# Attention and a gated MLP on one core: a new table of planned times, first loads placed one by one, and the last 128 tokens summed in two PSUM banks

## The chip, the cores and the metric

The kernel runs on one core of one Trainium2 chip. The metric is the device time of one execution in microseconds; the median of several executions counts. The engines are TensorE (PE; its weight loads are shown apart as PEld), VectorE (DVE), ScalarE (ACT), GpSimd (POOL) and SyncE (SP, which here only issues transfers).

## What is computed

Windowed causal attention (each position sees itself and the 63 before it), then a two-layer MLP whose hidden layer is gated by the sigmoid of a convolution of three taps along the sequence. Batch 8, 8 heads, 576 positions, 64 per head; 512 model columns, 1024 hidden ones.

```python
def _attn_ref(q, k, v):                       # q, k, v: 8 x 8 x 576 x 64
    scores = np.matmul(q, k.transpose(0, 1, 3, 2)) / np.sqrt(D)
    mask = (rel >= 0) & (rel < 64)            # rel = query position - key position
    scores = np.where(mask, scores, -1e9)
    scores = scores - np.max(scores, axis=-1, keepdims=True)
    attn = np.exp(scores)
    attn = attn / (np.sum(attn, axis=-1, keepdims=True) + 1e-09)
    return np.matmul(attn, v)

def _moe_ref(x, w_in, conv_w, w_out):         # x: 8 x 576 x 512
    h = np.maximum(x @ w_in, 0.0)             # w_in: 512 x 1024
    conv_out = sum(conv_w[k] * shifted(h, k - 1) for k in range(3))
    gate = 1.0 / (1.0 + np.exp(-conv_out))
    return h * gate @ w_out                   # w_out: 1024 x 512
```

The three MLP weights arrive as 64-bit floats; the kernel reads them as pairs of 32-bit words and makes 32-bit floats of them itself.

## The kernel before

**Units.** The 4608 tokens are worked off in 12 units (`NU`) of 384 tokens. For each unit PE does, in this order of dependence:

- *scores* (`qk`, L375): k and q of six blocks of 64 tokens. In the first two units the score blocks are 64 rows high, from the third on 32. A batch of the later units is 64 or 128 pairs of weight load and multiply as the trace counts them; DVE adds the mask and takes the row maximum (`row_max`, L382), ACT does the exponentials (`exps`, L392), then the rows are normalised (L403);
- a transpose of the probabilities (first two units on PE, L408, copied out by ACT, L413; later units on DVE, L429, and through transfers `ub<-T`, L441);
- *values* (`values`, L527): four groups per unit, each 12 matmuls in the program and 24 in the trace (a 32-bit matmul takes two passes), into one of three PSUM banks `acc`. ACT and DVE then split the sum into a rounded high part `xh` (L531) and a remainder `xl` (L534), and only after that is the bank free;
- the *first layer* (`mm1`, L547): per hidden block `f` of 128 (8 per unit) 12 matmuls of 384 columns (high by high, low by high, high by low, over four slices), into an `acc` bank; ACT takes the positive part (`relu`);
- the convolution and the gate on ACT and DVE (L582 to L616), two hidden blocks at a time;
- the *second layer* (`mm2`, L624): per hidden block 9 matmuls of 512 columns, three for each 128 tokens (`o` = 0, 1, 2), each `o` with a bank `po` of its own in which all eight hidden blocks are summed.

**The stream on PE.** In the steady part mm1 of unit u and mm2 of about two units back alternate, 12 matmuls and 9, and the scores and values of later units are put between them.

**The start.** SP issues the loads of k and q of unit 0, of v, and the weight words (`bits`, 512 KB each). While PE waits at the start it runs fillers (`keep_busy`, L222): matmuls on a zero tile whose results nobody reads. Each weight piece is made into a 32-bit float by two ACT operations (L259, L264) and three or four on DVE (L260, L261, L265, L283).

**The end.** After the last mm2, the bank of `o` = 2 is copied out in two halves, one by DVE and one by ACT (L660), and SP issues one transfer for each (L661).

**What sets the order.** All work is entered in a list with `at(t, engine, cost, ...)`. `queued` (the planner, L58 on) then simulates the five engines with the given costs: among the ready works of an engine it takes the one with the smallest planned time `t`, and the order so found is the order in which the instructions are issued. The planned times come from the table `START` and from the unit's number. Where PE has nothing to do before 110 us of planned time, `queued` puts in as many fillers as it thinks fit into the gap. Nothing of the planner runs on the chip: its costs decide the order and the fillers alone.

## Time and profile before

| what | value |
|---|---|
| median of 3 runs | 508.39 us (508.06 to 509.17) |
| the profiled execution, its own time | 507.84 us |
| its span, first to last instruction | 506.1 us |
| PE busy | 497.7 us, 98% of the span, fillers counted |
| DVE busy | 368.6 us, 73% |
| ACT busy | 384.5 us, 76% |
| POOL busy | 92.3 us, 18% |
| granted TensorE clock | 1.000 |

A busy share counts fillers, and a matmul whose end overlaps the next counts once. So the share of PE says that PE hardly ever stands still, not that all it does is needed. The time that a stretch of PE costs is read from start to start: from the start of its first matmul to the start of the next stretch's first. In the chain of waits each row is a stretch of one kind (start, us, engine, tile, line, count).

### The profile page before, as it was taken

What the parts mean: (1) busy time and instruction counts of PE and PEld (TensorE: products, weight loads), DVE (VectorE), ACT (ScalarE), POOL (GpSimd) and SP (SyncE); (2) the same over time, 40 slices, a digit from 0 to 9 for tenths busy, and PEclk for the clock granted to TensorE, in tenths of its full rate; (3) what the DMA queues carried; (4) which work ended last, traced back from release to release, by engine and by line L of the source; (5) the groups of instructions that cost most, each with busy time, mean ns of one, the idle gap of its engine ahead of it and who ended that gap; (6) DMA issues with size and microseconds to landing.
All of it is one profiled execution on the core that took longest, in us unless ns stands there. A gap on an engine that the chain in (4) does not pass through costs nothing.

```text
span 506.1 us, 14072 instructions
## 1 busy us (share of the span) xinstructions
PE 497.7 (98%) x5428; PEld 445.5 (88%) x5428; DVE 368.6 (73%) x1079; ACT 384.5 (76%) x1012; POOL 92.3 (18%) x196
## 2 busy tenths in 40 slices
PE   9999999999999999999999999999999999999996
PEld 8888998989989989988988997998998998999885
DVE  4999999795796777767677676695877585454970
ACT  6999998969979869949958956966975984444750
POOL 7125321301121402102100420220210230000000
PEclk9999999999999999999999999999999999999999
DMA  8986833629127226316415522712720521100111
GB/s 289 384 314 220 319 112 110 221 72 321 35 67 280 91 68 239 114 48 219 152 48 177 188 55 92 268 50 82 278 56 18 194 60 31 63 0 1 63 64 62
DMA packets 28163, 69.89 MB, mean 138 GB/s; under 512 B 5696, under 2 KB 15680, under 8 KB 28096
## 3 DMA queue, kind: packets, MB, share of 16 engines
q1 hardware_dynamic: 28096, 68.99, 40.0%
q8 instruction: 43, 0.70, 0.6%
q14 instruction: 24, 0.20, 0.1%
HBM read 47.73 MB, written 9.44 MB: 113 GB/s over the span
## 4 chain that ended last, share of the span: by engine, by line
PE 84%; ACT 7%; DVE 4%; SPq 1%; DMA 1%; issue 1%; POOL 0%; ACTq 0%; POOLq 0%
PE po L624 36%; PE acc L547 36%; PE acc L527 6%; ACT s L392 4%; PE sc L375 3%; PE acc L375 2%; DVE s L382 1%; SPq L441 1%; DMA q<-in_q_dram 1%; ACT L392 1%; ACT c L582 1%; DVE T L261 1%; ACT L596 1%; DVE T L265 0%; DVE c L589 0%
## 5 line engine op out<-in xcount | busy, mean ns | idle before, releaser
L589 DVE SCALAR_TENSOR_TENSOR c<-hbuf,cw,c 128x384 f32<-128x384 f32 (+1 forms) x192 | 116.9, 657 | 26.3 <-ACT c L582 25.6
L547 PE MATMUL acc<-xh,wih 128*128 128x384 f32 x384 | 131.1, 341 | 1.0 <-DVE nm L382 1.0
L547 PE MATMUL acc<-xl,wih 128*128 128x384 f32 x384 | 129.4, 337 | 0.0
L547 PE MATMUL acc<-xh,wil 128*128 128x384 f32 x384 | 128.9, 336 | 0.0
L624 PE MATMUL po<-woh,gh 128*128 128x512 f32 x288 | 114.2, 397 | 0.0
L624 PE MATMUL po<-wol,gh 128*128 128x512 f32 x288 | 113.4, 394 | 0.0
L624 PE MATMUL po<-woh,gl 128*128 128x512 f32 x288 | 111.9, 389 | 0.0
L392 ACT ACTIVATE s<-s,nm 128x96 f32<-128x96 f32 (+2 forms) x288 | 105.4, 372 | 3.4 <-DVE nm L382 3.2
L547 PEld LDWEIGHTS acc<-xh,wih 128*128 128x128 f32 x384 | 72.1, 188 | 6.8 <-DVE nm L382 1.0
L547 PEld LDWEIGHTS acc<-xh,wil 128*128 128x128 f32 x384 | 72.1, 188 | 2.7
L547 PEld LDWEIGHTS acc<-xl,wih 128*128 128x128 f32 x384 | 72.1, 188 | 0.0
L403 POOL TENSOR_TENSOR s<-s,r 128x768 f32<-128x768 f32 x27 | 41.4, 1532 | 159.0 <-DVE r L398 116.5
L624 PEld LDWEIGHTS po<-woh,gl 128*128 128x128 f32 x288 | 54.1, 188 | 12.2
L601 DVE TENSOR_TENSOR c<-c,hbuf 128x768 f32<-128x768 f32 (+1 forms) x48 | 46.2, 963 | 22.3 <-ACT c L596 21.9
L624 PEld LDWEIGHTS po<-woh,gh 128*128 128x128 f32 x288 | 54.0, 187 | 9.6
L624 PEld LDWEIGHTS po<-wol,gh 128*128 128x128 f32 x288 | 54.2, 188 | 7.6
L576 ACT ACTIVATE hbuf<-acc 128x384 f32<-128x384 f32 x64 | 30.9, 486 | 38.4 <-PE acc L547 38.4
L582 ACT ACTIVATE c<-hbuf,cw 128x384 f32<-128x384 f32 (+1 forms) x96 | 53.8, 610 | 7.0 <-DVE gl L616 6.9
L616 DVE TENSOR_TENSOR gl<-c,gh 128x768 fp32r<-128x768 f32 x48 | 45.7, 952 | 16.2 <-ACT gh L613 16.0
L392 ACT ACTIVATION_READ_ACCUMULATOR s<-s,nm 128x1 f32 x288 | 55.5, 193 | 0.0
L613 ACT CAST gh<-c 128x768 fp32r<-128x768 f32 x48 | 39.8, 831 | 13.6 <-DVE c L601 7.9
L596 ACT ACTIVATE c<-c 128x768 f32<-128x768 f32 (+1 forms) x48 | 40.7, 847 | 3.9 <-DVE c L589 3.1
(72 smaller groups left out, 578.9 us busy)
## 6 DMA issues: line engine op xcount, KB each, us to landing
v<-in_v_dram SPq DMA_DIRECT2D x24, 768.0 KB, 6.5
ub<-T SPq DMA_DIRECT2D x240, 48.0 KB, 1.9
k<-in_k_dram SPq DMA_DIRECT2D x22, 448.0 KB, 6.1
q<-in_q_dram SPq DMA_DIRECT2D x22, 384.0 KB, 6.4
out_dram<-T SPq DMA_DIRECT2D x11, 768.0 KB, 3.6
bits<-in_w_in_dram SPq DMA_DIRECT2D x8, 512.0 KB, 7.8
bits<-in_w_out_dram SPq DMA_DIRECT2D x8, 512.0 KB, 4.1
k<-in_k_dram SPq DMA_DIRECT2D x2, 256.0 KB, 4.6
```

The lines of the kernel that those rows point to most:

```text
L392: nc.scalar.activation(x, x, AF.Exp, bias=nms[b][:, e], scale=-1.0, accum_out=sms[b][:, e])
L403: on.tensor_tensor(sv, sv, rs[b][:, e].unsqueeze(2).broadcast_to([P, e.stop - e.start, n]), ALU.mult)
L527: nc.tensor.matmul(acc[bank(("v", u, c))][h * D:(h + 1) * D, t * W:(t + 1) * W], vs[:, c, t, h], ub[g][:, 2 * p:2 * p + 2, 2 * t + h], sta ...
L547: nc.tensor.matmul(acc[bank(("m", u, f))][:, :NX], w[:, f, c], x[u % 2][:, c], start=(c == 0 and j == 0), stop=(c == NC - 1 and j == 2))
L576: nc.scalar.activation(hbuf[:, f, 1:1 + NX], ps[:, :NX], AF.Relu)
L582: nc.scalar.activation(cs[i % 2][:, a, :n], hbufs[u % 2][:, f, 1:1 + n], AF.Copy, scale=cw[:, 1, f:f + 1])
L589: nc.vector.scalar_tensor_tensor(c, hbufs[u % 2][:, f, e:e + n], cw[:, e, f:f + 1], c, op0=ALU.mult, op1=ALU.add)
L596: nc.scalar.activation(c, c, AF.Sigmoid)
L601: nc.vector.tensor_tensor(c, c, hbufs[u % 2][:, 2 * i:2 * i + 2, 1:1 + n], ALU.mult)
L613: nc.scalar.copy(halves(u, ghs[ring(u, i)]), kept(u, cs[i % 2]))
L616: nc.vector.tensor_tensor(halves(u, gls[ring(u, i)]), kept(u, cs[i % 2]), halves(u, ghs[ring(u, i)]).bitcast(F32), ALU.subtract)
L624: nc.tensor.matmul(po[t], x, w[:, f], start=(f == 0 and j == 0), stop=(f == NF - 1 and j == 2))
```

## The change

**The planner's model.** `queued` now counts how many PE instructions are waiting to be run: the kinds "tiled" (scores of the first two units and values) and "eight" (scores of the later units) use up a store of at most 170 units that fills up again at 12 per us; where the store is empty the planned end is put later. Some costs are lowered (ACT's weight operations, the copies, the gate), a few are raised, and the size put down for a load of k, q and v in the first units is smaller.

**The table.** All numbers of `START` are new. `sig`, `pv`, `ex`, `qk` and `mid` have a row more (units 0 to 3 and the rest), and `first` gives each of the four first pairs of k and q loads a time of its own.

**The last unit.** For `o` = 2 of the last unit, `mm2` is done in two halves of 256 columns, into the bank `po[2]` and the bank `sc[0]`. The last two hidden blocks are put in order of `o`: both blocks for `o` = 0, then both for 1, then both for the two halves of 2. DVE copies the half in `po[2]` and SP issues its transfer; ACT copies the half in `sc[0]` and issues that transfer itself.

```diff
@@ queued
-        end = free[e] = start + turn + x.cost * (1.75 if e == "PE" and start < WARM else 1.0)
+        end = start + turn + x.cost * (1.75 if e == "PE" and start < WARM else 1.0)
+        if e == "PE" and x.kind:
+            n = FEED[x.kind] * x.cost
+            fed = min(FEED_CAP, fed + (start - fed_at) * FEED_RATE)
+            end += max(0.0, (n - fed) / FEED_RATE - (end - start))
+            fed, fed_at = fed + (end - start) * FEED_RATE - n, end
+        free[e] = end
@@ START
-    "qk0": (-97.809, -91.941, -91.937, -96.905, -77.255, -53.129),
+    "first": (-93.058, -80.147, -81.455, -79.474),
+    "qk0": (-63.31, -62.834, -53.48, -26.846, -47.703, -53.065),
...
+FEED, FEED_CAP, FEED_RATE = {"tiled": 33, "eight": 78}, 170.0, 12.0
@@ load_qk
+                t = START["first"][2 * g + a] if u == 0 else t
...
-                       w=[(name, g, n) for n in range(i, j)], mb=(0.00145 if u == 0 else 0.00112) * (e.stop - e.start))
+                       w=[(name, g, n) for n in range(i, j)], mb=(0.0012 if u == 0 else 0.0009 if u == 1 else 0.00112) * (e.stop - e.start))
@@ to_f32 (the other costs are changed in the same way)
-        at(t, "ACT", 0.0009 * n + 0.2, lambda: nc.scalar.activation(x, hw.bitcast(F32), AF.Abs, scale=2.0 ** -112), r=kb, w=kt)
+        at(t, "ACT", 0.0009 * n + 0.11, lambda: nc.scalar.activation(x, hw.bitcast(F32), AF.Abs, scale=2.0 ** -112), r=kb, w=kt)
@@ mm2
-    def mm2(u, f, t):
+    def mm2(u, f, t, half=None):
...
+        ps, e = (po[t], slice(0, DM)) if half is None else last_part(half)
         for j, (x, w) in enumerate(((gh, woh), (gh, wol), (gl, woh))):
-            nc.tensor.matmul(po[t], x, w[:, f], start=(f == 0 and j == 0), stop=(f == NF - 1 and j == 2))
+            nc.tensor.matmul(ps[:, :e.stop - e.start], x, w[:, f, e], start=(f == 0 and j == 0), stop=(f == NF - 1 and j == 2))
+
+    def last_part(half):
+        return (po[TT - 1], sc[0])[half], slice(half * DM // 2, (half + 1) * DM // 2)
@@ moe
+                if u == LAST and f >= NF - 2:
+                    t = n0 + NF - 2 + START["lag"][min(u, 5)] + 0.5 + 0.02 * o + 0.004 * (f - NF + 2)
...
-                for eng, cost, cut, copy in (("ACT", 0.35, slice(0, DM // 2), nc.scalar.copy), ("DVE", 0.35, slice(DM // 2, DM), nc.vector.tensor_copy)):
-                    at(t + 0.05 * o, eng, cost, lambda cut=cut, copy=copy: copy(ot[:, TT - 1, cut], po[TT - 1][:, cut]), r=[("po", o)], w=[("ot", o, cut.start)])
-                    at(t + 0.05 * o + 0.01, "SP", 0.45, lambda cut=cut: nc.sync.dma_start(out[u, :, TT - 1, cut], ot[:, TT - 1, cut]), r=[("ot", o, cut.start)], mb=0.13)
+                for half, key, eng, copy in ((0, ("po", o), "DVE", nc.vector.tensor_copy), (1, ("sc", 0), "ACT", nc.scalar.copy)):
+                    ps, e = last_part(half)
+                    at(t + 0.05 * o + 0.01 * half, eng, 0.4, lambda e=e, ps=ps, copy=copy: copy(ot[:, o, e], ps[:, :DM // 2]),
+                       r=[key], w=[("ot", o, half)])
+                    issue, by = ((nc.sync, "SP"), (nc.scalar, "ACT"))[half]
+                    at(t + 0.05 * o + 0.01 * half + 0.005, by, 0.45, lambda e=e, issue=issue: issue.dma_start(out[u, :, o, e], ot[:, o, e]),
+                       r=[("ot", o, half)], mb=0.13)
```

What this does to the order is shown at three places. The first is SP, its first transfers, before:

```order
L273 DMA bits_102<-in_w_in_dram 128x1024
L304 DMA cbits<-in_conv_w_dram 128x48
L245 DMA k<-in_k_dram 128x2x192
L245 DMA q<-in_q_dram 128x2x128
L245 DMA k<-in_k_dram 128x2x256
L245 DMA q<-in_q_dram 128x2x256
L245 DMA k<-in_k_dram 128x2x192
L245 DMA q<-in_q_dram 128x2x128
```

And SP's first transfers now:

```order
L255 DMA k<-in_k_dram 128x2x192
L255 DMA q<-in_q_dram 128x2x128
L283 DMA bits_102<-in_w_in_dram 128x1024
L255 DMA k<-in_k_dram 128x2x192
L255 DMA q<-in_q_dram 128x2x128
L255 DMA k<-in_k_dram 128x2x256
L255 DMA q<-in_q_dram 128x2x256
L255 DMA k<-in_k_dram 128x2x256
```

The first small pair of k and q now goes ahead of the first weight piece, the second small pair goes ahead of the large ones, and the words of the convolution (`cbits`) come later.

The second place is PE in a unit of the steady part (`ub` holds the transposed probabilities, `sc` and `acc` are banks). Before, a batch of 128 score pairs is followed by one group of values and then the second layer; the other three groups follow 21 matmuls later:

```order
L375 MATMUL sc_105<-k,q 32x96
L375 MATMUL sc_106<-k,q 32x96
L527 MATMUL acc_109<-ub_61,v 64x64 x12
L624 MATMUL po_110<-woh,gh_97 128x512
L624 MATMUL po_110<-wol,gh_97 128x512
L624 MATMUL po_110<-woh,gl_100 128x512
```

Now the four groups of values stand together, and the batch of 128 score pairs (64 rows of the order) follows at once:

```order
L635 MATMUL po_112<-woh,gl_100 128x512
L537 MATMUL acc_108<-ub_61,v 64x64 x12
L537 MATMUL acc_109<-ub_61,v 64x64 x12
L537 MATMUL acc_107<-ub_62,v 64x64 x12
L537 MATMUL acc_108<-ub_62,v 64x64 x12
L385 MATMUL sc_105<-k,q 32x96
L385 MATMUL sc_106<-k,q 32x96
```

The first and the fourth group use the same bank. The batch of 64 score pairs, which followed the three groups before, now stands alone between mm1 and mm2 stretches. Six units have this form.

The third place is the end of PE's program, before (`po_110`, `po_111`, `po_112` are `o` = 0, 1, 2):

```order
L624 MATMUL po_110<-woh,gl_100 128x512
L624 MATMUL po_111<-woh,gh_97 128x512
L624 MATMUL po_111<-wol,gh_97 128x512
L624 MATMUL po_111<-woh,gl_100 128x512
L624 MATMUL po_112<-woh,gh_97 128x512
L624 MATMUL po_112<-wol,gh_97 128x512
L624 MATMUL po_112<-woh,gl_100 128x512
```

And now:

```order
L635 MATMUL po_111<-woh,gl_100 128x512
L635 MATMUL po_112<-woh,gh_97 128x256
L635 MATMUL po_112<-wol,gh_97 128x256
L635 MATMUL po_112<-woh,gl_100 128x256
L635 MATMUL po_112<-woh,gh_97 128x256
L635 MATMUL po_112<-wol,gh_97 128x256
L635 MATMUL po_112<-woh,gl_100 128x256
L635 MATMUL sc_105<-woh,gh_97 128x256
L635 MATMUL sc_105<-wol,gh_97 128x256
L635 MATMUL sc_105<-woh,gl_100 128x256
L635 MATMUL sc_105<-woh,gh_97 128x256
L635 MATMUL sc_105<-wol,gh_97 128x256
```

`o` = 1 is done twelve narrow matmuls before the end instead of three wide ones, and the last half has a bank of its own. Over the whole program PE has 44 fillers instead of 50 (rows of `keep_busy`, two passes each), 18 stretches of values instead of 27, and 840 wide and 48 narrow matmuls of the second layer instead of 864 wide ones.

More of the change, by code (lines that the diff above doesn't have):

```diff
@@ L97, in queued @@
             waiting[x.eng].append(x)
-    dma, port, order, left = 0.0, {"DVE": 0.0, "POOL": 0.0}, [], len(works)
+    dma, fed, fed_at = 0.0, FEED_CAP, 0.0
+    port, order, left = {"DVE": 0.0, "POOL": 0.0}, [], len(works)
     while left:
@@ L274, in weights @@
                 bits[buf][:, a * DM:(a + 1) * DM], src[f].bitcast(U32).rearrange("p (e two) -> p e two", two=2)),
-               w=[("bits", buf, a)], mb=0.52)
+               w=[("bits", buf, a)], mb=0.52 if key == "out" else 0.46)
         n = len(fs) * DM
@@ L279, in weights @@
         if key == "out":
-            at(t, "ACT", 0.0009 * n + 0.12, lambda: nc.scalar.copy(hi, x), r=kt, w=his)
+            at(t, "ACT", 0.00088 * n + 0.05, lambda: nc.scalar.copy(hi, x), r=kt, w=his)
         else:
-            two(t, "POOL", 0.00127 * n, lambda: nc.gpsimd.tensor_copy(hi, x), r=kt, w=his)
+            two(t, "POOL", 0.00105 * n, lambda: nc.gpsimd.tensor_copy(hi, x), r=kt, w=his)
         two(t, "DVE", 0.00104 * n + 0.07, lambda: nc.vector.tensor_tensor(lo, x, hi.bitcast(F32), ALU.subtract), r=kt + his, w=los)
@@ L477, in weigh @@
             at(t + 0.4, "PE", 0.66, lambda n=n: transpose_pe(u, n), r=[("s", b, n % 2 * 2), ("s", b, n % 2 * 2 + 1), "mask0"], w=m)
-            at(t + 0.5, "ACT", 0.55, lambda n=n: untile(u, n), r=m, w=[("u", g, i) for i in range(4)])
+            at(t + 0.5, "ACT", 0.47, lambda n=n: untile(u, n), r=m, w=[("u", g, i) for i in range(4)])
     def softmax(u, b, t, ex_at):
@@ L498, in softmax @@
             at(t, "DVE", 0.15, lambda: guard(b, e, nc.vector), w=sw)
-        at(t, "DVE", 0.15, lambda: reciprocal(b, e), r=sw, w=[("r", b, i) for i in range(NB)])
+        at(t, "DVE", 0.12, lambda: reciprocal(b, e), r=sw, w=[("r", b, i) for i in range(NB)])
         if u < 3:
@@ L537, in attend @@
         g, x = c // 2, u % 2
-        at(t, "PE", 0.72, lambda: values(u, c), r=[("v", g)] + [("u", g, i) for i in range(4)], w=[("acc", ("v", u, c))],
+        at(t, "PE", 0.735, lambda: values(u, c), r=[("v", g)] + [("u", g, i) for i in range(4)], w=[("acc", ("v", u, c))],
            kind="tiled")
-        at(t + 0.1, "ACT", 0.4, lambda: split_hi(u, c), r=[("acc", ("v", u, c))], w=[("xh", x, c)])
+        at(t + 0.1, "ACT", 0.375, lambda: split_hi(u, c), r=[("acc", ("v", u, c))], w=[("xh", x, c)])
         at(t + 0.2, "DVE", 0.48, lambda: split_lo(u, c), r=[("acc", ("v", u, c)), ("xh", x, c)], w=[("xl", x, c)])
@@ L634, in moe @@
                    w=[("acc", ("m", u, f))])
-            at(n + 0.3, "ACT", 0.4, lambda f=f: relu(u, f), r=[("acc", ("m", u, f))], w=[("h", y, f)])
+            at(n + 0.3, "ACT", 0.385, lambda f=f: relu(u, f), r=[("acc", ("m", u, f))], w=[("h", y, f)])
             for o in range(TT):
-                at(n + START["lag"][min(u, 5)] + 0.5 + 0.01 * o, "PE", 0.683, lambda f=f, o=o: mm2(u, f, o),
-                   r=[("gh", ring(u, f // 2)), ("gl", ring(u, f // 2)), f"out{f}h", f"out{f}l"],
-                   w=[("po", o)])
+                t = n + START["lag"][min(u, 5)] + 0.5 + 0.01 * o
+                if u == LAST and f >= NF - 2:
+                    t = n0 + NF - 2 + START["lag"][min(u, 5)] + 0.5 + 0.02 * o + 0.004 * (f - NF + 2)
+                r = [("gh", ring(u, f // 2)), ("gl", ring(u, f // 2)), f"out{f}h", f"out{f}l"]
+                if u == LAST and o == TT - 1:
+                    for half in range(2):
+                        at(t + 0.01 * half, "PE", 0.36, lambda f=f, o=o, half=half: mm2(u, f, o, half), r=r,
+                           w=[(("po", o), ("sc", 0))[half]])
+                    continue
+                at(t, "PE", 0.683, lambda f=f, o=o: mm2(u, f, o), r=r, w=[("po", o)])
         for i in range(NF // 2):
```

62 lines of the change are left out of this document (31 added, 31 removed), and 6 rows, old and new, of the table START.

## The prediction

> **What bounds the kernel now.** I read the page's busy shares first, then the busy time by stretches, then PE's own rows from start to start, and the chain of waits for the steady part.
>
> ```profile
> span 506.1 us, 14072 instructions
> PE 497.7 (98%) x5428; PEld 445.5 (88%) x5428; DVE 368.6 (73%) x1079; ACT 384.5 (76%) x1012; POOL 92.3 (18%) x196
> ...
> q8 instruction: 43, 0.70, 0.6%
> ```
> ```profile
> 0.00:20.00 20.00, 18.19 (x219) 16.59 (x220) 12.56 (x66) 15.05 (x60) 10.72 (x46) 1.00 0.91 331
> 20.00:40.00 20.00, 19.37 (x310) 16.79 (x307) 19.89 (x69) 18.63 (x58) 4.19 (x7) 1.00 0.84 297
> 40.00:60.00 20.00, 19.24 (x363) 17.68 (x364) 19.93 (x73) 19.25 (x73) 10.14 (x15) 1.00 0.84 305
> ```
> ```profile
> L222 PE MATMUL acc<-spare 128*128 128x112 f32 x78 | 12.3, 317 | 1.1 <-DVE spare L225 1.1
> L222 PE MATMUL po<-spare 128*128 128x112 f32 x12 | 2.2, 296 | 0.0
> L222 PE MATMUL sc<-spare 128*128 128x112 f32 x10 | 1.6, 293 | 0.0
> ```
>
> In the second fence the columns are stretch, length, busy time of PE, PEld, DVE, ACT, POOL, clock, share and rate of the transfers. PE is the bound, so three things can save time: gaps on PE, fillers that stand for gaps, and what PE loses between kinds of matmul. The fillers (100 rows, 12.3 + 2.2 + 1.6 = 16.1 us) lie nearly all in the first 40 us, where DVE is full from 20 us on (19.89 and 19.93 of 20) and ACT nearly so.
>
> ```profile
> 274.98 2.30 PE acc L547 x12
> ...
> 306.00 0.79 PE acc L527 x21
> 306.79 1.06 issue
> 307.86 0.33 PE acc L527 x3
> ...
> 315.73 2.31 PE acc L547 x12
> ...
> 351.99 2.25 PE acc L527 x72
> 354.24 0.93 PE sc L375 x58
> 355.17 2.31 PE acc L547 x12
> 357.47 2.06 PE po L624 x9
> 359.53 2.11 PE acc L547 x12
> ```
>
> The chain of waits (start, us, what, rows) shows the steady part. From 315.73 to 355.17 one unit takes 39.44 us. The unit before took 40.75 us (274.98 to 315.73), and the 1.31 us more are one gap inside a group of values, where PE waited for nothing but its own instructions ("issue"). Everywhere else PE runs without a break from about 47 us to the last matmul at 501.70.
>
> **The change part by part.** The terms are against the profiled execution, 507.84 us, which lies 0.55 us under the median of the runs (508.39).
>
> *The start.*
>
> ```profile
> 0.74 0.38 SPq L273 DMA_DIRECT2D bits<-in_w_in_dram  x1
> ...
> 1.64 0.43 SPq L245 DMA_DIRECT2D k<-in_k_dram  x1
> ...
> 4.40 0.67 ACT L259 ACTIVATE T<-bits 128x512 f32<-128x512 f32 x1 [2.38 <-DMA bits<-in_w_in_dram]
> ...
> 5.07 0.68 ACT L264 ACTIVATE bits<-bits 128x512 uint32<-128x512 uint32 x1
> ...
> 6.18 0.57 PE L375 MATMUL sc<-k,q 64*64 64x64 f32 x16 [0.17 <-DMA q<-in_q_dram]
> ...
> 7.17 0.35 ACT L392 ACTIVATE s<-s,nm 128x64 f32<-128x64 f32 x1 [1.30 <-DVE nm L382]
> ```
> ```profile
> bits<-in_w_in_dram SPq DMA_DIRECT2D x8, 512.0 KB, 7.8
> ```
>
> The first scores start when the first q has landed, behind 512 KB of weights. Now that pair goes first: 512 KB less at 331 GB/s (first stretch) is **1.6 us** earlier. PE's program agrees: six fillers fewer, 12 rows of 0.16 us (16.1 us over 100), 1.9 us. ACT gains less. Its first weight operation still stands ahead of the first exponentials, and its words now land behind k and q, by about 1.0 us (128 x 2 x 192 and 128 x 2 x 128 floats are 320 KB, at the same rate; or two issues of 0.43 us), so it ends near 6.1; exponentials start about 1.0 us before 7.17, and the second weight operation (0.68 us), which had lain in idle time, now lies among them: 0.4 us gained. The ends are 0.4 and 1.9 us. I take 1.6, because PE's rows are what ends here, and because DVE, idle for 7.4 of the first 20 us, can start its full stretch as much earlier.
>
> *Stretches of values.* 72 rows take 2.25 us (351.99 to 354.24); 48 take 1.55:
>
> ```profile
> 88.41 1.55 PE acc L527 x48
> ```
>
> So 24 rows cost 0.70 us and each stretch 0.15 us besides. Nine stretches fewer (18 for 27) save 1.35 us, and one return to wide matmuls less saves its surplus, 2.31 against 2.11, 0.2 us: **1.5 us**. The number of excursions from the wide matmuls per steady unit is unchanged, so nothing more comes of it. From below this is 0: the fourth group of values now needs the bank of the first, and waits if ACT's and DVE's split takes over 2.25 us.
>
> *Instructions for PE.* Blocks of instructions are brought by the transfers of q8 (packets, MB, share): 43 for 2 x 5428 rows, so some 256 each. I counted PE's instructions in program order (a 32-bit matmul is two loads and two multiplies): the one that came late at 307.86 is number 7618. Blocks then begin at 7618 plus or minus multiples of 256. The block before it began 46 instructions into the scores, at about 304.65. So a block needs up to 3.2 us from the start of the one before; 128 score pairs and 24 value pairs had used up the 256 in 2.1 us. Another place bounds it from below:
>
> ```profile
> 106.95 0.85 PE acc L527 x24
> 107.80 0.93 PE acc L375 x58
> 108.73 0.74 PE sc L375 x52
> 109.47 0.90 PE po L624 x3
> 110.37 2.09 PE acc L547 x12
> ```
>
> There a block begins 12 instructions into the scores (107.9) and the next in the third first-layer matmul (110.9): 3.0 us, no gap. In the new order six units run 96 value pairs and 128 score pairs in one piece, about 455 instructions in 2.95 + 1.70 us. A block begins 65, 185, 31, 133, 235 and 81 instructions into the piece, and its 256 are used up after 2.8, 1.8, 3.1, 2.25, 5 and 2.65 us. With 2.95 us per block PE waits 0.15 + 1.15 + 0 + 0.7 + 0 + 0.3 = 2.3 us; with 3.2 us it is 3.4 us. From below it may be nothing, if blocks come faster than the one that stalled. [...] The old gap of 1.3 us goes, so the term is **+1.0** (-1.3 to +2.1).
>
> [...]
>
> *The halves of the last 128 tokens.* Twenty-four matmuls of 512 columns (2.06 / 9 = 0.229 us) become 48 of 256. The two widths of the trace, 384 (2.11 / 12 = 0.176) and 512, give 0.0004 us a column and so 0.122 us: 48 x 0.122 - 24 x 0.229 = **+0.3**. If a narrow one cost as much as one of 384 columns, it would be +2.9; below nothing there is no reason, since no column is left out.
>
> *The end.*
>
> ```profile
> 501.44 0.69 DVE L666 COPY T<-po 128x512 f32<-128x512 f32 x1 [8.49 <-PE po L624]
> 502.13 0.42 DVE L660 COPY T<-po 128x256 f32<-128x256 f32 x1
> 502.59 0.91 SPq L661 DMA_DIRECT2D out_dram<-T  x2
> 502.64 0.37 ACT L660 COPY T<-po 128x256 f32<-128x256 f32 x1 [1.26 <-DVE T L660]
> ```
>
> ACT's half waited for DVE's copy of the same bank and SP issued the two transfers one after the other. With a bank and a queue of its own ACT's copy starts with the last matmul, at 502.13 in these terms in place of 502.64: **-0.5**. If ACT's queue takes longer to issue than SP's 0.45 us this shrinks to about 0; with the wide copy of `o` = 1 also done sooner it is -0.8.
>
> The other lowered costs are numbers of the planner; they add no instruction. The sum is -1.6 - 1.5 + 1.0 + 0.3 - 0.5 = **-2.3**: 505.5 us for 507.84, and 506.1 us against the median.
>
> **The rivals.**
>
> *Blocks are never late.* There was one gap in 27 stretches of values, which speaks for it; its size against the count of instructions speaks against. The six waits of 2.3 us go: 503.8 us.
>
> *The start is ACT's.* Only 0.4 of 1.6 us is gained: 507.3 us. For it speaks that ACT is busy for 18.63 and 19.25 us of the stretches from 20 us on; against it, that PE's gaps up to 47 us end on DVE:
>
> ```profile
> 40.31 0.45 PE L547 MATMUL acc<-xh,wih 128*128 128x384 f32 x1 [0.78 <-DVE nm L382]
> ```
>
> *Values come too early for their input.* At 150.26 the values start in the very moment in which the last `ub<-T` lands.
>
> ```profile
> 148.52 1.74 DMA ub<-T
> ...
> 150.26 0.92 PE acc L527 x24
> ```
>
> Pulled ahead by one step of PE (2.11 + 2.06 us) there, they would wait. Half a step in one unit is 2.1 us: 508.2 us, no difference to see. The other units show no such link.
>
> *Late blocks, slower.* The rival on the other side: with v, k and q loaded at the same time, a block takes longer than in the one gap of before. At 4.0 us per block the six pieces wait 1.2 + 2.2 + 0.9 + 1.75 + 0 + 1.35 = 7.4 us, 5.1 more than I take: 511.2 us, slower. It decides from about 3.65 us per block on, where the waits come to 5.6 us. For it speaks that the new pieces are the longest yet; against it, the block that came in 3.0 us or less.
>
> **How the numbers follow.** The forecast (506.1 us, own range 504.5 to 507.3) gets 0.50; blocks never late 0.13; the start with ACT 0.14; values too early 0.13; slow blocks 0.10. A measurement of this kernel can tell about 0.2%, 1 us, from no change, so faster is below 507.4: nearly all of the first, the second, half of the third, 0.68; the same: the other half, most of the fourth and a little of the first, 0.20; slower: the fifth and some of the fourth, 0.12. The range reaches from all terms at their good ends short of both extremes (503.2) to the late values with the upper end of late blocks (509.4).
>
> **What would show it.** First scores near 4.6 us and fewer filler rows; a steady unit of 39.3 us where no block is late, and longer by 0.3 to 1.2 us in the first, second, fourth and sixth of the six units, as "issue" in the scores behind four groups of values; second-layer rows of 256 columns at about 0.12 us; ACT's last copy right behind the last matmul and the span's end 3.5 us after it instead of 4.0. It would be wrong if PE shows waits for DVE, ACT or `ub<-T` after 60 us, or if first-layer matmuls start later than before in spite of the earlier scores.

## The result and the profile after

The changed kernel takes **516.39 us** (median of 6 runs, 511.74 to 519.42); the kernel before took 508.53 beside it. The ratio is 1.0134 (1.0085 to 1.0184): slower by 1.3%, where 506.1 us and faster were forecast. The median lies outside the range of 503.2 to 509.4. A second series of the same kernel gave 517.13 us and 1.0136 (1.0102 to 1.0171). One execution of each series, 519.42 and 520.66 us, counts as slow (over 1.5% above the fastest of its series) and is left out of the ratios; that of the second series is the one profiled there. The profiled execution of the first series took 516.17 us, with a span of 514.4 us.

Page of the changed kernel, the lines on the engines and the instruction blocks:

```profile
span 514.4 us, 14039 instructions
PE 500.3 (97%) x5440; PEld 448.7 (87%) x5440; DVE 364.8 (71%) x1079; ACT 362.2 (70%) x994; POOL 86.4 (17%) x196
...
q8 instruction: 43, 0.70, 0.6%
```

PE has 12 rows more than before and is busy for 97% of the span (98% before); the page as a whole doesn't say where 8 us went. The waits of PE behind 60 us do, in part (us in total, times, longest):

```profile
PE acc L385 <- issue: 3.7, 2, 3.3
PE acc L537 <- DMA ub<-T: 1.2, 1, 1.2
```

The first is the late instruction block, the second the values that come too early. Before there was one `issue` of 1.06 us there and no `ub<-T`. The chain of waits of the changed kernel around the longer gap, and the steady unit behind it:

```profile
224.60 2.95 PE acc L537 x96
227.55 0.86 PE sc L385 x52
...
228.48 0.67 PE acc L385 x41
229.14 3.33 issue
232.47 0.37 PE acc L385 x7
232.84 3.84 PE po L635 x9
...
348.29 2.95 PE acc L537 x96
351.24 0.86 PE sc L385 x52
...
355.18 2.06 PE po L635 x9
...
387.48 2.95 PE acc L537 x96
```

Two things stand there. In the second of the six pieces (a piece is the stretch of 96 value pairs with the 128 score pairs behind it) PE runs no instruction for 3.33 us (`issue`). And the nine second-layer matmuls behind it take 3.84 us in this chain (3.75 from the start of the first to the start of what follows, 232.77 to 236.52), not 2.06. The busy time by stretches says why (the columns are stretch, length, PE, PEld, DVE, ACT, POOL, granted clock, share and GB/s of the transfers):

```profile
224.00:228.00 4.00, 4.00 (x143) 3.68 (x147) 1.67 (x3) 2.33 (x5) 0.00 (x0) 1.00 0.22 46
228.00:232.40 4.40, 1.14 (x96) 0.94 (x84) 1.97 (x17) 3.55 (x15) 0.00 (x0) 1.00 0.86 297
232.40:236.50 4.10, 4.03 (x16) 3.12 (x16) 1.51 (x16) 3.76 (x21) 0.00 (x0) 0.58 0.60 236
236.50:240.00 3.50, 3.50 (x79) 3.04 (x78) 0.25 (x3) 0.49 (x1) 0.00 (x0) 1.00 0.00 0
```

The gap falls where v, k and q land (0.86 of the transfer engines), and behind it the granted clock is 0.58 on the mean: the trace's clock records have it at half from 233.03 to 236.44 us. The fifth unit, where no block is late, shows the plan as it was meant: 348.29 to 387.48 is 39.2 us.

The start of the changed kernel, from the timelines of ACT and PE (start, duration, engine, line, operation, and in brackets the idle time and what ended it):

```profile
6.90 0.66 ACT L269 ACTIVATE T<-bits 128x512 f32<-128x512 f32 x1 [4.88 <-DMA bits<-in_w_in_dram]
7.46 0.33 ACT L402 ACTIVATE s<-s,nm 128x64 f32<-128x64 f32 x1
```
```profile
8.01 0.92 PE L385 MATMUL sc<-k,q 64*64 64x64 f32 x16 [0.80 <-DVE T L270]
```

The first scores do come early, at 3.88 us (6.18 before). But ACT waits 4.88 us for weight words that now land at 6.9, its weight operation stands ahead of the exponentials, and these begin at 7.46 (7.17 before). PE's second scores wait until 8.01 (this row names DVE; in the second profile of this kernel, below, the same wait of 0.6 us is put down to the load of q) and take 0.85 us from start to start, where 16 such pairs took 0.50 before: 1.7 times as long. The clock records show the full clock only from **14.58 us** on; before it was 5.33. Up to 14.4 us the filler rows follow each other every 0.21 us, from 15.9 us on every 0.11 us (before, every 0.21 us up to 5.24 and every 0.11 us from 5.40 on), so ahead of the first record PE ran at about half the clock. As a measure of the whole start serves the first long run of first-layer matmuls with nothing between them: it began at 54.39 us before and begins at 56.49 now. Ahead of it stand the same rows of values, transposes and first-layer matmuls in both kernels, and 64 score pairs and 10 filler rows fewer now.

The end, from the timeline and the transfers of the changed kernel (KB each, median us to landing):

```profile
508.73 0.28 PE L635 MATMUL sc<-woh,gl 128*128 128x256 f32 x1
...
509.10 0.37 ACT L682 COPY T<-sc 128x256 f32<-128x256 f32 x1 [2.21 <-PE sc L635]
509.50 2.38 ACTq L685 DMA_DIRECT2D out_dram<-T  x1
```
```profile
out_dram<-T SPq DMA_DIRECT2D x1, 128.0 KB, 2.0
out_dram<-T ACTq DMA_DIRECT2D x1, 128.0 KB, 3.8
```

ACT's copy does stand right behind the last matmul. Then ACT needs 2.38 us to issue its transfer, where SP's rows of the same size take 0.37. From the start of the last matmul to the end of the span it is 5.6 us (508.73 to 514.35); before it was 4.4 (501.70 to 506.05).

### The profile page after: what moved, and what is told of

It reads as the page before. It is cut to its first block, busy times and chain, and to the rows that moved or that the text cites. A ratio compares the mean times of both kernels' runs of the same rounds, so it can differ in the third digit from the quotient of the medians.

```text
span 514.4 us, 14039 instructions
## 1 busy us (share of the span) xinstructions
PE 500.3 (97%) x5440; PEld 448.7 (87%) x5440; DVE 364.8 (71%) x1079; ACT 362.2 (70%) x994; POOL 86.4 (17%) x196
## 4 chain that ended last, share of the span: by engine, by line
PE 85%; DVE 6%; ACT 3%; DMA 3%; issue 1%; SPq 1%; POOL 0%; ACTq 0%
PE po L635 38%; PE acc L557 34%; PE acc L537 6%; PE sc L385 3%; ACT s L402 2%; PE acc L385 1%; DMA bits<-in_w_out_dram 1%; DVE s L392 1%; DVE T L275 1%; DMA bits<-in_w_in_dram 1%; DVE T L271 1%; PE acc L231 1%; DVE s L413 1%; DVE T L270 1%; ACT T L269 1%
## 5 line engine op out<-in xcount | busy, mean ns | idle before, releaser
L599 DVE SCALAR_TENSOR_TENSOR c<-hbuf,cw,c 128x384 f32<-128x384 f32 (+1 forms) x192 | 108.3, 620 | 14.1 <-ACT c L592 14.1
L635 PE MATMUL po<-wol,gh 128*128 128x512 f32 (+1 forms) x288 | 113.2, 393 | 0.0
L635 PE MATMUL po<-woh,gh 128*128 128x512 f32 (+1 forms) x288 | 113.2, 393 | 0.0
L635 PE MATMUL po<-woh,gl 128*128 128x512 f32 (+1 forms) x288 | 111.7, 388 | 0.0
L413 POOL TENSOR_TENSOR s<-s,r 128x768 f32<-128x768 f32 x27 | 39.9, 1477 | 138.2 <-ACT s L402 70.1
L586 ACT ACTIVATE hbuf<-acc 128x384 f32<-128x384 f32 x64 | 30.9, 485 | 45.5 <-PE acc L557 45.4
L592 ACT ACTIVATE c<-hbuf,cw 128x384 f32<-128x384 f32 (+1 forms) x96 | 53.5, 609 | 7.4 <-DVE gl L626 7.3
L611 DVE TENSOR_TENSOR c<-c,hbuf 128x768 f32<-128x768 f32 (+1 forms) x48 | 46.0, 961 | 14.4 <-ACT c L606 14.0
L402 ACT ACTIVATION_READ_ACCUMULATOR s<-s,nm 128x1 f32 x288 | 54.3, 188 | 0.0
L392 DVE CUSTOM_DVE_ANT_0 s<-sc,mask 128x96 f32<-128x96 f32 (+2 forms) x180 | 34.1, 254 | 26.9 <-PE sc L385 26.8
```

Of the source, the lines that this page charges most:

```text
L392: nc.vector.tensor_tensor_reduce(out=ss[b][:, i, h, o:n], in0=bank_of(u, b, i, h)[:, o:n], in1=mask[m][:, o:n], scale=-0.125, scalar=3.0e3 ...
L402: nc.scalar.activation(x, x, AF.Exp, bias=nms[b][:, e], scale=-1.0, accum_out=sms[b][:, e])
L413: on.tensor_tensor(sv, sv, rs[b][:, e].unsqueeze(2).broadcast_to([P, e.stop - e.start, n]), ALU.mult)
L586: nc.scalar.activation(hbuf[:, f, 1:1 + NX], ps[:, :NX], AF.Relu)
L592: nc.scalar.activation(cs[i % 2][:, a, :n], hbufs[u % 2][:, f, 1:1 + n], AF.Copy, scale=cw[:, 1, f:f + 1])
L599: nc.vector.scalar_tensor_tensor(c, hbufs[u % 2][:, f, e:e + n], cw[:, e, f:f + 1], c, op0=ALU.mult, op1=ALU.add)
```

## The experiments

Theory after this: the plan loses time in five places (the first clock, ACT's order at the start, the values near 76 us, late blocks with half a clock behind them, ACT's issue), and each is to be had back alone. The rival: a busy start and a full PE row hide these, and the time went elsewhere. All edits are made to the changed kernel; each series was run beside the kernel before (medians 508.4 to 508.8 us).

### Fillers in the first gaps

```diff
             if n > 0 and clean:
+                gaps += 1
+                n += {1: 1, 2: 7, 3: 4}.get(gaps, 0)
```

> Twelve more filler matmuls in the first three gaps of TensorE's row (1, 7 and 4 more); no other instruction changes. Theory (a cold TensorE): in the changed kernel the granted clock was full only from 14.6 us, in the kernel before from 5.3 us, and the long run of index matmuls began at 56.5 us. With the gaps filled the clock is full by about 6 us, the long run begins near 53.5 us, and the time falls by about 3 us, from 516.4 to 513.4. Rival (the start hangs on ScalarE, which waits 4.9 us for the bits that land at 10.2 us): the clock comes early, the long run still begins after 55.5 us, and the time stays within 1 us of 516.4.

Measured: 515.82 us (1.0154, 1.0125 to 1.0183). The full clock came at 7.3 us, but the long run began at 55.84, not 53.5: the seven fillers of the second gap ran on past the landing of q, and the second scores began at 9.01. The rival's time came true. (The 10.2 us in the rival's text are the time from issue to landing of `cbits`; the weight words land at 6.9 us.) Something else was learned: twelve fillers are 48 instructions, so every border of a block lies 48 instructions earlier in its piece. The border that lay 185 instructions into the second piece now lies at 137 there, and one lies at 187 in the fifth (235 - 48). The gap moved with it (waits, and stretches of this kernel):

```profile
PE acc L387 <- issue: 3.5, 1, 3.5
```
```profile
345.00:349.70 4.70, 1.25 (x106) 1.03 (x93) 2.01 (x18) 2.26 (x6) 0.00 (x0) 0.88 0.88 296
349.70:355.40 5.70, 5.70 (x21) 5.17 (x21) 1.51 (x16) 1.00 (x4) 0.19 (x1) 0.50 0.40 160
```

Nothing near 229 us, 3.5 us near 346, and 6.8 us of half a clock behind it (348.60 to 355.42). So here the border's place in the piece decided which one stalled, as the prediction had it; the loads that land there (0.88 of the transfer engines) belong to it too, as the third edit shows (5.1 us for a block under v's load, 2.9 without it).

### SP issues the last half

```diff
-                    issue, by = ((nc.sync, "SP"), (nc.scalar, "ACT"))[half]
+                    issue, by = ((nc.sync, "SP"), (nc.sync, "SP"))[half]
```

> Only the engine that issues the last half's transfer changes: SyncE for ScalarE. Theory (ScalarE's issue of 2.38 us is the price): the issue takes 0.4 to 0.5 us and the landing 2.0 us as in SyncE's other rows, and from the start of the last matmul to the end of the span it takes 3.5 to 4.0 us, where it took 5.6 us; the time falls by 1.3 to 2.1 us. Rival (a second transfer on SyncE's queue stands behind the first half's, or the write's own completion takes that long from any queue): over 5 us from the last matmul to the end, and the time within 0.5 us of 516.4.

Measured: 514.26 us (1.0105, 1.0070 to 1.0139).

```profile
507.93 0.28 PE L635 MATMUL sc<-woh,gl 128*128 128x256 f32 x1
508.00 1.03 SPq L685 DMA_DIRECT2D out_dram<-T  x2
508.30 0.37 ACT L682 COPY T<-sc 128x256 f32<-128x256 f32 x1 [2.21 <-PE sc L635]
```

SP issues both halves in 1.03 us, and the span ends at 512.4: 4.5 us behind the start of the last matmul, 1.2 less than with ACT. ACT's issue ended 3.2 us behind that start (509.50 + 2.38), SP's second one 1.1; of these 2.1 us 1.2 reach the end of the span. The 2.1 us between the medians are not this alone: in this profile, with the same instructions on PE, the full clock came at 6.8 us and the long run began at 53.77, 2.7 us earlier, while the waits put down to `issue` come to 6.3 us in place of 3.7. The range of 3.5 to 4.0 us was missed: the bank of its own brings nothing against the 4.4 us of before. SP's second issue does end earlier than before (1.1 us behind the start of the last matmul for 1.8), but the span does not; why is not shown.

### v behind k and q

```diff
-            load_v(n0 + NF - 0.3, u + 2)
+            load_v(n0 + NF + 0.3, u + 2, [("q", 0, 1)] if u + 3 < NU else ())
```

(`load_v` reads the keys in the list, so the planner may not put it ahead of that q.)

> The two transfers of v of each later unit (1.5 MB) are put behind those of k and q in SyncE's queue; in one unit a batch of 32 scores changes places with 24 value matmuls. Theory A (the block of instructions was late because 1.5 MB of v had begun to land): the gap of 3.6 us in the scores near 229 us goes to 1.3 us or less, no clock of 0.5 follows it, and the time falls by about 4 us (2.3 to 3.3 of the gap, 1.7 of the half clock), to 512.4. Theory B (the position of the block's border in the dense piece is enough): the gaps stay in the second and the fourth of the six pieces, 2.5 us or more in the second, and the time stays within 1.5 us of 516.4.

Measured: 513.38 us (1.0091, 1.0072 to 1.0111). Waits, and the stretch of the second piece:

```profile
PE acc L537 <- ACT hbuf L583: 2.4, 1, 2.4
PE acc L385 <- issue: 2.0, 2, 1.1
```
```profile
228.00:232.40 4.40, 3.31 (x130) 2.69 (x112) 3.67 (x34) 3.55 (x13) 0.00 (x0) 1.00 0.51 165
```

The gap near 229 us is 1.1 us in place of 3.3, and no half clock follows; the fourth piece waits 0.9 us in place of 0.4. Both theories are right in part: with its border at the same place the second piece stalls in both runs, for 3.33 us with v's load beside it and for 1.09 without. Counted in the trace, the block before the late one begins 185 instructions into the piece, at 227.4 us in the changed kernel, and PE goes on at 232.47: **5.1 us** for a block. Here it is 227.6 to 230.46: **2.9 us**. The transfer of the block itself takes about 1 us in both (0.95 and 1.24); it starts at 230.22 in the changed kernel, 2.8 us after the border, and at 227.82 here, 0.2 us after it.

But PE waited 2.4 us for the values near 74 us (the row names ACT; in the next run the same wait names `ub<-T`), and half a clock followed, from 77.5 to 80.9 us. The third unit's v is now issued right behind k and q, and lands beside the twelve `ub<-T`, which take SP 11.35 us where they took 8.45 in the changed kernel.

### The three together

> The three edits together. If the cold start, the late blocks with their half clock and ScalarE's issue are what the change lost: 516.4 - 3.0 - 4.0 - 1.6 = 507.8 us, and what is left above the forecast of 506.1 is the wait of 1.2 us for the weights' transpose near 77 us. If only the first falls: about 513. If the losses hide one another (a later bound takes the place of each): 511 or more.

Measured: 513.47 us (1.0086, 1.0061 to 1.0110). The profiled run was the best of six, 510.21 us, with the full clock from 4.7 us on and no half clock later; the wait near 76 us was 2.3 us there too. The sum of the three edits did not come, the last of the three cases (511 or more) did. One edit makes a wait of its own, and with the fillers the long run began at 54.63 where it began at 53.77 and 53.88 with the other two edits alone. This profile, 3.3 us under the median, does not show what the other executions lost.

### The weights behind the first softmax

In this edit and the ones below works are moved after planning, so that nothing else is planned anew: `put_behind(order, moved, last)` takes works out of the order and puts them behind `last`; a work that needs one of them follows it.

```diff
+        order = put_behind(order, of(order, "SP", ("bits", 0, 0))[:1], of(order, "SP", ("q", 1, 1))[0])
+        order = put_behind(order, of(order, "ACT", ("bits", 0, 0))[:1], of(order, "ACT", ("sm", 1, 1))[0])
```

> The first 512 KB of weights are issued behind the first eight transfers of k and q in place of third, and their conversion stands behind the first ten exponentials on ScalarE (four rows on VectorE move with it); TensorE's order is the changed kernel's. Theory (the start is ScalarE's: exponentials could not begin before 7.3 us because ScalarE waited 4.9 us for the weights, and the second scores waited until 7.9 us for a q queued behind them): exponentials begin near 5.5 us, the second scores near 6.5 us, the first transposes of TensorE start near 14.8 us (16.0 in the run with SyncE's issue, 18.7 in the changed kernel's), and the time falls by about 1.2 us beside what the clock at the start does. Rival (the start hangs on the other loads): the transposes stay at 15.8 us or later with the clock full by 7 us.

Measured: 518.68 us (1.0205, 1.0180 to 1.0229), worse.

```profile
5.24 0.35 ACT L426 ACTIVATE s<-s,nm 128x64 f32<-128x64 f32 x1 [3.23 <-DVE nm L416]
```
```profile
PE po L442 <- DVE r L432: 4.8, 1, 4.8
```

The theory's steps came: exponentials from 5.24 us, second scores at 6.57, first transposes at 14.49. Then PE waited 4.8 us. The weights' conversion stood on POOL and DVE ahead of the last normalisation and held it up, and the clock was at half behind that gap too, from 19.5 to 26.4 us. So ACT's order is what stood against the early scores, but the work pushed aside there is in the way 10 us later.

### The values near 76 us later

```diff
+        order = put_behind(order, pe[i + 3:i + 5] + pe[i - 3:i - 1], pe[i - 1])
```

(`pe[i - 3:i - 1]` are the two groups of values at 76.72 us, `pe[i - 1]` the 64 scores, `pe[i + 3:i + 5]` twelve first-layer matmuls.)

> Only TensorE's order between 75 and 82 us changes: two groups of values stand behind a group of 64 scores and 12 first-layer matmuls in place of ahead of them. Theory (the values came 1.2 us too early for ub<-T): no wait of TensorE over 0.3 us between 70 and 84 us, and 0.3 to 1.2 us less time (2.5 less where the wait brought a stretch of half clock): 515 to 516. Rival (gl<-c of VectorE, ready at 77.3 us, is next): the wait moves to the second-layer matmuls, and the time stays.

Measured: 513.52 us (1.0102, 1.0075 to 1.0130). Between 60 and 100 us no wait of PE is left: the wait of 1.2 us was the values' place. The time fell by 2.9 us, more than the 0.3 to 1.2 us forecast; in this profile the full clock came at 6.0 us and the long run began at 53.67, so the edit alone is not what was measured. The gap of the second piece came again (3.57 us from 224.8 on), with half a clock from 227.9 to 234.7.

### The pieces split

```diff
+            if x.kind == pe[i - 1].kind == "eight" and pe[i - 2].kind == "tiled" == pe[i - 5].kind:
+                order = put_behind(order, [x], pe[i + (2 if pe[i + 1].w[0][0] == "acc" else 3)])
```

> In the six units with 96 value pairs and 128 score pairs in one piece the second 64 score pairs stand behind the next 12 first-layer or 9 second-layer matmuls; no other instruction moves. Theory (the piece uses up instructions faster than blocks of 256 come): after 100 us no gap over 0.7 us in TensorE's row, no half clock there, six more changes between small and wide matmuls at 0.15 us: -3.6 - 0.6 - 1.7 + 0.9 = -5.0, 511.4 us. Rival (v's load alone makes a block late, whatever the piece): a gap of 2 us or more near 229 us stays, and the time stays within 1.5 us of 516.4.

Measured: 512.08 us (1.0081, 1.0054 to 1.0109), the best of the single edits. Waits of this kernel after 60 us, and the stretch of the second piece:

```profile
PE acc L409 <- issue: 1.1, 1, 1.1
PE acc L581 <- DVE xl L568: 1.0, 4, 0.2
```
```profile
228.00:232.40 4.40, 4.00 (x94) 3.42 (x94) 1.86 (x19) 4.18 (x23) 0.00 (x0) 1.00 0.68 236
```

One gap is left, 1.1 us in the second piece under v's load, and there is no half clock behind the start in this profile. Here too the full clock came early, at 5.8 us. First-layer matmuls now wait for DVE's split in four units, 1.0 us in all, so the split costs more than the 0.9 us of its changes.

### These edits together, twice

The fourth kernel of this set has the weights, the values, the split and SP's issue:

> The three edits of this set together with SyncE's issue of the last half: 516.4 - 1.2 - 1.0 - 5.0 - 1.2 = 508.0 us, and 2.7 less where the first full clock comes by 7 us in place of 14.6: 505.3. If it ends below 506.5, the plan was worth what was forecast and lost it in these places; if it stays at 508.5 or above, one of the edits does not do what its theory says, and its own profile shows which.

Measured: 514.59 us (four runs; 1.0118, 1.0103 to 1.0133). The weights' edit cost its 4.8 us again and half a clock at 24 us; from 30 us on there was no gap over 1.0 us.

Then the weights' conversion was put behind the last normalisation of the first unit on all engines, and v's loads behind those of k and q, once with the split and once without:

```diff
+        order = put_behind(order, first, [x for x in of(order, "DVE", ("r",)) if x.w[0][0] == "s"][3])
...
+            later = [y for y in sp[sp.index(x):sp.index(x) + 8] if y.w and y.w[0][0] == "q"]
+            order = put_behind(order, [x], later[-1]) if later else order
```

> Five edits: the weights' first transfer and conversion behind the first softmax (this time also on VectorE and GpSimd, so that the last normalisation does not wait behind it), the values near 76 us later, the pieces split, v's loads behind those of k and q, SyncE's issue of the last half. Theory: first transposes near 14.5 us and the long run near 52.3 us with the clock full by 7 us (-1.3 beside the runs with an early clock), no wait for ub<-T, no gap over 0.7 us and no half clock after 60 us, 4.4 us from the last matmul to the end: 505 to 506 us, below the kernel before. If v's loads in their new place make other blocks late, gaps of about 1 us stay and the time is 508 or more.

> The same five edits without the split of the pieces. If v's loads alone make blocks late in the merged pieces, this is 0.9 us below the version with the split (six changes of 0.15 us fewer): 504 to 505. If the merged piece outruns its blocks even with v's loads behind it, one or two gaps of 0.6 to 1.5 us stay and it is level with the split version or up to 1.5 us above.

Measured: 517.33 us (1.0152, 1.0129 to 1.0176) with the split, 514.12 (1.0101, 1.0070 to 1.0132) without; both forecasts were missed by some 10 us. The waits of the first of the two:

```profile
PE sc L409 <- DVE nm L416: 2.5, 1, 2.5
PE acc L561 <- ACT hbuf L607: 2.5, 1, 2.5
PE acc L561 <- ACT ub L447: 1.5, 1, 1.5
...
PE sc L409 <- issue: 0.3, 1, 0.3
```

In the steady part every gap over 0.6 us is gone. But the moved conversions once more make PE wait, 2.5 + 1.5 us between 21 and 30 us, and the third unit's v lies beside `ub<-T` again; the clock is at half behind both, from 30.9 to 34.3 and from 82.1 to 85.5 us. The long runs began at 59.3 and 58.6 us. Without the split, gaps of 1.1 to 1.4 us stay in the second piece and near 130 us. Two attempts at the start failed: where the clock came early, moving the weights brought the first transposes to 14.5 and 14.8 us, 1.2 to 1.5 us earlier than in the run with SP's issue (15.95), and it loses more on what the conversions then stand ahead of.

### The changed kernel once more

> The changed kernel once more, unaltered. If the late first clock (14.6 us in its profile, 5.8 to 6.8 us in four runs with the same instructions on TensorE at the start) is an accident of one execution, this profile shows the full clock before 8 us, the long run near 53.8 us, and a time of 513 to 515; the gap near 228 us with half a clock behind it comes again. If it belongs to the kernel, the clock is full after 10 us again and the time is 516 or more.

Measured: 517.13 us. In its profile the full clock came at 14.56 us again, the long run at 56.37, and the longest gap in the second piece:

```profile
PE acc L385 <- issue: 3.9, 2, 3.5
PE sc L385 <- issue: 3.5, 5, 1.5
PE acc L537 <- DMA ub<-T: 1.3, 1, 1.3
```

So the late clock came twice. But the runs with SP's issue, the later v, the later values and the split have the same instructions on PE up to 50 us, and there it came at 5.8 to 6.8 us. Both happen; the last section shows in what these executions differ. The second row names a loss that the prediction had no term for: of its 3.5 us 1.5 stand at 197.7 us, in a batch of 64 score pairs behind the first piece, and 1.0 at 400.5, in one behind the sixth. In the run with SP's issue the first of these came too (1.2 us at 193.3).

### Five repairs, without touching the weights

Two fillers more in the second gap, the values later, v behind k and q from the fourth unit on, the split in the second and fourth piece only, SP's issue:

```diff
+                n += 2 * (gaps == 2)
...
+                if piece in (2, 4):
```

> The changed kernel with five repairs: two fillers more in the gap of 1.0 us before the second scores, the values near 76 us later, v's loads of the fourth and later units behind those of k and q (the third unit's stays, since its early load held up ub<-T), the split in the second and fourth of the six pieces only, and SyncE's issue of the last half. Theory: full clock by 8 us, long run near 53.7 us, no wait over 0.7 us and no half clock between 60 and 500 us, 4.4 us at the end. From the profile of the version with all six pieces split: 508.5 - 1.3 (its gap near 227 us) - 1.2 (end) - 1.3 (four splits less) = 504.7 of span, 506.5 us, below the kernel before by 2 us. If late blocks come elsewhere, 508 to 510.

Measured: **508.19 us** (median of 12, 506.76 to 510.06); the ratio to the kernel before is 0.9990 (0.9975 to 1.0004). Its waits after 60 us:

```profile
PE sc L411 <- issue: 0.8, 2, 0.6
PE acc L563 <- DMA ub<-T: 0.5, 1, 0.5
PE acc L583 <- DVE xl L570: 0.2, 1, 0.2
```

The wait near 76 us is 0.5 us with the third unit's v in its old place. The 8.2 us are back. Against the changed kernel's profile they lie at the start, in the steady part and at the end: the long run begins at 53.83 us in place of 56.49 (2.7), the last matmul at 501.71 in place of 508.73 (another 4.4), and the span ends 4.4 us behind it in place of 5.6 (1.2): 8.3, from 514.4 to 506.1 us. That it stays level with the kernel before, not 2 us below, is measured; the forecast of 506.5 for this kernel missed as the first one did. The 2.7 us at the start are not shown to come from a repair: the window at whose end the full clock came here (2.83 to 6.24 us) was over before PE came to the two fillers, and four runs without them had a clock as early. The share of each other repair was not taken apart.

## Why the prediction was wrong

**The start, -1.6 us: this step failed.** "I take 1.6, because PE's rows are what ends here." The first scores were 2.3 us early, and nothing behind them was. Exponentials wait on ACT behind a weight operation whose words land at 6.9 us. The step put that operation's end near 6.1 us and gave the end at which only 0.4 us is gained as a rival ("the start is ACT's"). With the clock at full by 7 us the long run began at 53.8 us, 0.6 earlier than before and with 64 score pairs (0.9 us) less done: +0.3 us in place of -1.6. When the clock was late it was +3.0. Two signs that the prediction named for being wrong came true: a wait for `ub<-T` after 60 us, and first-layer matmuls that start later than before (30.24 us, and 27.53 in the run with SP's issue, for 24.37).

**The first clock was not in the prediction at all.** It counted "six fillers fewer" as time saved. PE now stands idle for 1.0 to 1.2 us before the second scores, and in both profiles of the changed kernel the full clock came 9.2 us later than before. Four runs with the same instructions on PE up to 50 us had the full clock at 5.8 to 6.8 us, so the gap alone does not make it late; the last section shows in what these executions differ.

**Stretches of values, -1.5 us: right.** The 96 pairs take 2.95 us in every piece without a gap, 0.15 us less for each stretch saved, and a steady unit takes 39.2 us, where 39.3 was expected.

**Instruction blocks, +1.0 us: gaps came at two of the places counted, and the term was mis-sized.** It measured +2.6 us (3.3 + 0.4 less the old gap of 1.1), and 1.7 more of half a clock behind it. The 2.3 us of waits in the +1.0 are those at the lower of two estimates, 2.95 us per block; the choice was the author's, and no run shows these waits: the changed kernel's profile has 3.3 and 0.4 us in their place. Gaps came in the second and the fourth piece, as counted from the borders (0.4 us in the fourth, where 0.7 was expected; none over 0.1 in the first and the sixth in this profile). "With 2.95 us per block" held where nothing else lands: 2.9 us in the run with v later, where the share of the transfer engines is 0.00 from 228.1 to 229.1 us. Under v's load a block took 5.1 us: more than the rival of late blocks allowed, 4.0. Its deciding point, 3.65 us, was passed in one piece only, but the half clock behind the gap added 1.7 us (3.75 for 2.06, start to start), which no term and no rival had. Had blocks never been late, as the first rival has it, there would have been no gap; all nine profiles with the six pieces unsplit show one of 1.1 us or more.

**The halves, +0.3 us: right.** Narrow matmuls follow each other every 0.12 us (508.49, 508.61, 508.73; 0.118 on the mean of these, where 0.122 was taken), which makes it +0.2.

**The end, -0.5 us: this step failed.** It was +1.2 us. The step named the condition, "if ACT's queue takes longer to issue than SP's 0.45 us", but bounded its price at "about 0"; 2.38 us of issue make it a loss. With SP's issue the end is level with before (4.5 for 4.4 us), so the 0.5 us did not come either way.

**Values too early: the rival came true as well**, by 1.2 us near 76 us; the prediction had looked at 150 us for it.

Put together for the profiled execution: start +3.0, values -1.5, wait for `ub<-T` +1.2, late blocks +3.3 + 0.4 - 1.1 (the old gap), half clock +1.7, halves +0.2, end +1.2: +8.4 us, beside 8.3 us of span (514.4 - 506.1). Each of these is read or worked out from rows of the two profiles; that they add up is arithmetic, and it holds for this execution. What the other ten executions of the changed kernel lost, and whether their first clock was late, no trace shows.

## What to carry to other kernels

A plan that makes PE's row denser can bring out waits for instruction blocks, loads and copies that the looser one did not have (here 3.3 and 0.4 us at the borders of blocks and 1.2 us for `ub<-T`, where one wait of 1.06 us stood before): before merging stretches of small matmuls, look at what is being loaded there and count where a block of instructions ends (some 256 here, an estimate from 43 transfers for 2 x 5428 rows). A gap on PE can cost more than its length: in these profiles every one of 2.6 us or more was followed by 3.4 or 6.8 us at half the clock, one of 2.35 us was and one of 2.54 was not, and the half clock behind the gap of 3.3 us cost 1.7 us more; so price a stall with that. An earlier first load was worth only what the engine behind it could start earlier (first scores at 3.88 us for 6.18, exponentials at 7.46 for 7.17), and a transfer issued from another queue costs its issue time there (2.38 us on ACT, 0.37 on SP), which has to be seen in a row first.

## What the runs showed of the hardware

The clock, from the clock records of all profiles (us; a "gap" is a distance between one start and the next in PE's and PEld's rows behind 8 us, given from 2.3 us on; the half clock after the last matmul is left out):

```
kernel                  full clock from   gaps (length at start)       half clock
before                  5.3               none                         none
changed                 14.6              3.57 at 228.9                233.0 to 236.4
changed, once more      14.6              3.71 at 231.6                236.4 to 239.8
fillers                 7.3               3.70 at 346.0                348.6 to 355.4
SP issues               6.8               3.82 at 226.8                232.1 to 235.5
v later                 5.8               2.62 at 73.6                 77.5 to 80.9
three together          4.7               2.54 at 74.3                 none
weights last            5.9               5.00 at 16.4, 3.44 at 230.2  19.5 to 26.4, 234.6 to 238.0
values later            6.0               3.57 at 224.8                227.9 to 234.7
split                   5.8               none                         none
weights, values, split  10.3              5.00 at 18.6                 23.9 to 27.4
with v later, split     10.4              2.75 at 26.7, 2.69 at 79.0   30.9 to 34.3, 82.1 to 85.5
with v later, no split  6.5               2.71 at 24.9, 2.35 at 78.3   27.0 to 33.8, 81.6 to 85.0
five repairs            6.2               none                         none
```

Half the clock lasted 3.4 us or twice that. Each gap of 2.6 us or more was followed by it, one of 2.35 was, one of 2.54 was not, and none under 2 us.

The trace goes further than lengths. All changes of the clock in one profile lie on one grid of 3.413 us: in the changed kernel 14.58, 233.03 and 236.44 are 64 steps and one step apart. Where the grid lies differs from execution to execution. PE's row, cut into the windows of that grid, goes in all 14 profiles with what the clock did at the end of each. The first four windows of the changed kernel, and one window each of the run without the split and of the three edits together (columns as above; PE's busy time as the trace counts it):

```profile
0.92:4.34 3.42, 3.29 (x24) 3.09 (x28) 0.08 (x1) 1.09 (x1) 2.84 (x13) 1.00 0.69 158
4.34:7.75 3.41, 2.86 (x22) 2.26 (x14) 0.96 (x9) 0.85 (x3) 2.69 (x12) 1.00 0.91 304
7.75:11.16 3.41, 3.15 (x26) 2.75 (x26) 2.35 (x11) 3.23 (x17) 2.97 (x8) 1.00 1.07 390
11.16:14.58 3.42, 3.42 (x39) 2.94 (x38) 2.14 (x17) 1.80 (x9) 0.67 (x6) 1.00 1.04 417
```
```profile
78.17:81.58 3.41, 1.27 (x61) 1.08 (x46) 3.41 (x5) 2.71 (x5) 0.00 (x0) 1.00 0.21 54
```
```profile
72.93:76.35 3.42, 1.63 (x69) 1.16 (x67) 3.39 (x5) 3.42 (x5) 1.26 (x3) 1.00 0.28 72
```

(The clock column says 1.00 in the first four lines because there is no record ahead of the first change; the filler rows follow each other every 0.21 us up to 14.4 us, and every 0.11 us from 15.9 us on.) The full clock came at the end of the first window that PE filled, the fourth here (3.42 of 3.42 us). In all 14 profiles it came 27 times, always behind a window that PE was busy for to the end, and never behind one of 97% or less (27 such windows at half clock). The clock fell to half behind every window with at most 1.58 of 3.41 us of PE (19 times, the windows that hold the last matmul counted), and behind none with 1.62 or more up to the last matmul. So the gap of 2.35 us, which lay in one window (1.27 us of PE left), had half a clock behind it, and that of 2.54 us, shared by two (1.63 us left in the first), had none.

This is how the changed kernel's late first clock lies to the grid. In both of its profiles the grid lies so that a window runs from 4.34 (4.32) to 7.75 (7.74) us and holds most of the idle time before the second scores, which begins at 7.2; the ones before and after it aren't filled either. In the four profiles with the same start the filled window ends at 5.80 to 6.79, ahead of the idle time. Moved over the changed kernel's own row, about one position of the grid in six has no filled window before 7.2 us (an estimate from that row). That both of its profiles fell there looks like chance, but is not shown to be: no run sets the grid's position, and those of the two, 0.92 and 0.91 us, are nearly the same, while the other twelve profiles lie between 0.05 and 3.38.

One transfer issued by ACT, the only one of the kernel on that queue, took 2.38 us to issue in the changed kernel, and SP's of the same size 0.37 us. Whether it is the first one on a queue or every one was not tried.

A block of instructions whose transfer takes 1 us began that transfer 0.2 us after its border without other transfers and 2.8 us after it under v's load (0.71 to 0.87 of the transfer engines from 227.4 to 230.2 us). What held it up there, the trace does not show.
